# Transposing the first half of even x on TensorE, taking FFN1 part by part, pairing 64-row remainders, moving a diagonal product to VectorE, and loading the gate's x early

## The chip, the cores and the metric

One core of one Trainium2 chip. The metric is the device time of one execution in microseconds (us). Medians are over all runs of a kernel; ratios are explained with the result. "PE" is TensorE (matmuls), "PEld" its weight loads, DVE is VectorE, ACT is ScalarE, POOL is GpSimd, and SP and ACT issue the DMAs. The span of a profile is a little shorter than the time (160.6 us of span for a run of 162.38 us).

## The reference, cut to what matters

```
x: [2048, 448]; g = sigmoid(sum(x * gate_w))          # one gate per row
a = y + x * Dskip        # y: a complex state-space scan, h[t] = Lam*h[t-1] + Bu[t], y = 2 Re(h C)
b = silu(x @ w1) @ w2    # w1: [448, 1792], w2: [1792, 448]
out = g * a + (1 - g) * b
```

448 is 3*128 + 64. So every product that contracts over 448 columns needs three full matmuls and a fourth one with only 64 useful rows, "the remainder". The kernel splits the 2048 rows into even and odd ones. FFN1 (x @ w1, then silu) is done in four chunks of 512 rows: chunks 0 and 1 are even rows, 2 and 3 odd rows. A chunk has 14 blocks of 128 columns of w1.

## The kernel before

The program records operations for each engine with the buffers they read and write, and derives the semaphore waits from them. Each engine runs its own operations in the order given.

```python
# first half of even x: a transposing DMA on SP (XTe0); w1 in column pieces on ACT's queue
ld("act", W1E[:, 0:3, 0:384], ..., "W1Eb")
ld("act", W1E[0:64, 3, :], B_w1[384:448, :], "W1Ea")
...
ldt(XT[:, 0:4, 0:512], x2[0:512, 0:512], "XTe0")
...                                        # later the second half (XTe1), odd x (XTo0, XTo1)
T.op("pool", lambda e: e.memset(W1E[64:128, 3, :], 0.0), writes=["W1Ez"])   # pads the remainder

def ffn1(c, fb, mm_only=False, act_only=None):      # one block, banks 0..3 in turn
    ...
    for j in range(4):                               # j = 3: the remainder, 128 rows of which 64 are zero
        ins = pe.matmul(ps[:, bank, :], W[:, j, fb * 128:(fb + 1) * 128],
                        XT[:, j0 + j, h * 512:(h + 1) * 512], start=(j == 0), stop=(j == 3))
    ...                                              # then ACT: AT = silu(bank)

warm(10)                                             # matmuls on zeros, to bring the clock up
first = [ffn1(0, fb, mm_only=True) for fb in range(2)]
T.op("pe", mm_cols, ...)                             # small vectors into columns, for the P chain on DVE
...
def ytile(kt, odd):                                  # an output tile: 7 matmuls, plus
    if odd:                                          # D*x as a product with diagonal matrices DO
        pe.matmul(ps[:, bank, 0:64], XT[:, 3, t0:t0 + 128], DO[:, 0, 64:128], start=False, stop=False)
        for j in range(1, 4):
            lo = 64 + (j - 1) * 128
            ins = pe.matmul(ps[:, bank, lo:lo + 128], XT[:, 3 + j, t0:t0 + 128], DO[:, j, :], ...)
    ...                                              # DVE: out = bank * g + (1-g)*FFN2
...
# gate: gate_w and all of x are loaded on SP, after the seven LT transposes; 16 reductions on DVE
# order on PE: FFN1 of chunks 0, 1; BU (scan inputs); FFN2 of 0; FFN1 of 2; FFN2 of 1; FFN1 of 3;
#              FFN2 of 2; K0 (needs CO from DVE); FFN2 of 3 and the output tiles
```

Names in the traces: BB and Y hold the rows of B (Y the last 64 of them), LT is B scaled and transposed, BU its product with x, HS the scan's inputs and states. CE and CO are C scaled for even and odd outputs. K0 is CO times BB plus a diagonal of D, by which x enters an even row directly; it is kept in KT. GT is the gate, JK the scratch of its reductions. The P chain is a row of small DVE operations that compute coefficients.

## Time and profile before

| before | |
|---|---|
| time, first median of 3 runs | 161.24 us (161.21 to 162.41) |
| span of the profile | 160.6 us |
| PE busy | 153.4 us, 96% |
| DVE, ACT busy | 68%, 42% |
| PE without a gap | 14.10 to 157.53 us |

The page's engine totals and the shares of the chain of waits (the chain that ended last, followed back):

```profile
PE 153.4 (96%) x772; PEld 73.8 (46%) x772; DVE 108.6 (68%) x216; ACT 67.7 (42%) x111; POOL 7.3 (5%) x16
...
PE 92%; DMA 4%; ACT 2%; DVE 1%; issue 0%
```

PE is the bottleneck, and not only by its share: the chain that ends last is 92% PE. The timeline of PE at the start (start and duration in us, then engine, line, operation, count; in brackets the idle time before and what ended it):

```profile
1.25 4.45 PE L299 MATMUL ps<-Q 128*128 128x512 bf16 x10 [1.25 <-DVE SG L211]
7.13 3.57 PE L275 MATMUL ps<-XT,W1E 128*128 128x512 bf16 x8 [1.43 <-DMA XT<-in_A_x_dram]
10.64 0.25 PE L292 MATMUL ps<-ID,R 3*128 3x3 bf16 x4
10.82 1.90 PE L275 MATMUL ps<-XT,W1E 128*128 128x512 bf16 x8
14.10 20.89 PE L275 MATMUL ps<-XT,W1E 128*128 128x512 bf16 x96 [1.39 <-ACT AT L283]
```

PE waits for x until 7.13 us, its first 8 FFN1 matmuls take 446 ns each, and after 16 it waits for ACT. From 14.10 us it runs at 217.6 ns a matmul (20.89/96). I read the 446 ns, about twice that, as a lowered TensorE clock ("cold"). The profile's granted clock reads 1.00 there, so this is inferred. So the kernel starts "as if" at 14.10 - 16*0.2176 = 10.6 us. I call this the effective start.

The chain of waits in the middle and around the first output tiles (start, duration, what):

```profile
66.74 12.09 PE ps L275 x56
78.83 10.59 PE ps L553 x56
89.42 0.18 PE ps L497 x4
89.60 12.19 PE ps L275 x56
...
122.83 1.32 PE ps L664 x7
124.16 0.03 PE ps L667
124.19 0.17 PE ps L671 x3
```

L275 with 56 matmuls is FFN1 of an odd chunk, L553 the FFN2 between, L497 the columns of D; L664 are the 7 matmuls of an odd tile, L667 and L671 its D*x, 0.20 us. Around the one group of K0 whose weights have only 64 columns, the timeline of PE shows what a change of the array's shape costs:

```profile
116.31 0.22 PE L586 MATMUL ps<-DE,ID 128*128 128x128 bf16 x1
116.46 1.51 PE L584 MATMUL ps<-CO,BB 128*64 128x448 bf16 x7
117.81 0.19 PE L586 MATMUL ps<-DE,ID 128*64 128x64 bf16 x1
117.93 2.82 PE L553 MATMUL ps<-W,AT 128*128 128x448 bf16 x14
```

A 128-column matmul streams for about 0.06 us, yet the next starts 0.15 us later when the shape changes; the 64-column one streams for 0.03 us and the next starts 0.12 us later. That is 0.09 us each way. Last, one of DVE's waits (who waited for whom: us in total, times, longest):

```profile
DVE JK L520 <- DMA W1O<-in_A_x_dram: 7.7, 1, 7.7
```

This is the gate waiting for its x in the middle of DVE's work (33.6 to 41.2 us).

### The profile page before, as it was taken

The page shows a single profiled execution, that of the slowest core. Times are in us where ns is not written, and L with a number is a line of the kernel's source. Part 1 is how long each engine was busy: PE and PEld are TensorE (multiplying, and loading weights), DVE is VectorE, ACT ScalarE, POOL GpSimd, SP SyncE. Part 2 cuts the span into 40 slices and gives each one's busy share as a digit, 9 for nine tenths or more (in the row PEclk, how much of TensorE's full clock was granted, in tenths as well). Part 3 has the DMA queues.
Part 4 walks back from the last instruction along what each step waited for, and adds up shares of the span by engine and source line. Part 5 has one row for each costly group of instructions (what it writes and reads, how often), then busy time and mean ns, then how long its engine had stood idle before and what let it go on. Part 6 is the DMA issues. An engine that isn't in the chain of part 4 may idle for free.

```text
span 160.6 us, 2016 instructions
## 1 busy us (share of the span) xinstructions
PE 153.4 (96%) x772; PEld 73.8 (46%) x772; DVE 108.6 (68%) x216; ACT 67.7 (42%) x111; POOL 7.3 (5%) x16
## 2 busy tenths in 40 slices
PE   6696999999999999999999999999999999999992
PEld 2132444444444455444455444455555555555551
DVE  0027999930799999999999999999941131133341
ACT  3019769999587610766522476331421101100000
POOL 7500000000003000000000000000000000000000
PEclk9999999999999999999999999999999999999999
DMA  5996979799930730026930000000000100102211
GB/s 109 297 354 142 213 142 119 121 149 395 323 82 4 255 145 0 0 63 107 116 69 0 0 0 0 4 2 0 0 0 0 61 30 27 57 0 88 87 57 57
DMA packets 26787, 14.76 MB, mean 92 GB/s; under 512 B 19861, under 2 KB 26010, under 8 KB 26778
## 3 DMA queue, kind: packets, MB, share of 16 engines
q1 hardware_dynamic: 25498, 13.03, 34.3%
q10 hardware_dynamic: 1280, 1.61, 3.3%
q8 instruction: 6, 0.10, 0.2%
q14 instruction: 3, 0.02, 0.0%
HBM read 7.92 MB, written 1.84 MB: 61 GB/s over the span
## 4 chain that ended last, share of the span: by engine, by line
PE 92%; DMA 4%; ACT 2%; DVE 1%; issue 0%
PE ps L275 30%; PE ps L553 26%; PE ps L664 13%; PE ps L569 13%; DMA XT<-in_A_x_dram 4%; PE ps L675 4%; PE ps L584 3%; PE ps L671 1%; ACT L340 1%; ACT P L334 0%; DVE OT L683 0%; ACT AT L283 0%; PE ps L667 0%; ACT JK L340 0%; PE ps L586 0%
## 5 line engine op out<-in xcount | busy, mean ns | idle before, releaser
L553 PE MATMUL ps<-W,AT 128*128 128x448 bf16 x224 | 43.5, 353 | 0.0
L283 ACT ACTIVATE AT<-ps 128x512 bf16<-128x512 f32 x56 | 32.5, 596 | 10.6 <-PE ps L275 10.3
L553 PEld LDWEIGHTS ps<-W,AT 128*128 128x128 bf16 x224 | 21.7, 98 | 20.1 <-issue 0.2
L683 DVE SCALAR_TENSOR_TENSOR OT<-ps,GT,LT 128x448 bf16<-128x448 f32 x16 | 10.9, 684 | 29.0 <-PE ps L675 22.3
L275 PE MATMUL ps<-XT,W1E 128*128 128x512 bf16 x112 | 26.4, 397 | 2.8 <-DMA XT<-in_A_x_dram 1.4
L558 ACT ACTIVATE LT<-ps,GT 128x448 bf16<-128x448 f32 x16 | 9.9, 634 | 43.6 <-PE ps L553 35.3
L275 PE MATMUL ps<-XT,W1O 128*128 128x512 bf16 x112 | 24.5, 379 | 0.0
L569 PE MATMUL ps<-XT,LT 128*128 128x512 bf16 x98 | 21.3, 379 | 0.0
L275 PEld LDWEIGHTS ps<-XT,W1E 128*128 128x128 bf16 x112 | 11.1, 101 | 17.6 <-POOL KT L250 2.3
L275 PEld LDWEIGHTS ps<-XT,W1O 128*128 128x128 bf16 x112 | 10.9, 98 | 12.9
L605 DVE TENSOR_TENSOR_SCAN G<-P,Q 128x1024 f32<-128x1024 f32 x7 | 15.7, 2276 | 0.0
L569 PEld LDWEIGHTS ps<-XT,LT 128*128 128x128 bf16 x98 | 9.6, 98 | 11.6
L520 DVE SCALAR_TENSOR_TENSOR JK<-W1O,GWB 128x448 bf16<-128x448 bf16 x16 | 8.8, 621 | 7.7 <-DMA W1O<-in_A_x_dram 7.7
L664 PE MATMUL ps<-CE,HS 128*128 128x448 bf16 x56 | 11.9, 353 | 0.0
L664 PE MATMUL ps<-CO,HS 128*128 128x448 bf16 x56 | 11.9, 352 | 0.0
L573 ACT ACTIVATE HS<-ps 128x512 bf16<-128x512 f32 x14 | 8.2, 596 | 5.1 <-PE ps L569 4.5
L602 DVE TENSOR_TENSOR Q<-G,SIN 128x1024 bf16<-128x1024 f32 x7 | 8.5, 1219 | 0.0
L602 DVE TENSOR_TENSOR Q<-G,COS 128x1024 bf16<-128x1024 f32 x7 | 8.5, 1210 | 0.0
L664 PEld LDWEIGHTS ps<-CO,HS 128*128 128x128 bf16 x56 | 5.5, 98 | 5.1
L675 PE MATMUL ps<-KT,XT 128*128 128x448 bf16 x32 | 7.4, 352 | 0.0
L664 PEld LDWEIGHTS ps<-CE,HS 128*128 128x128 bf16 x56 | 5.3, 98 | 4.4
L584 PE MATMUL ps<-CO,BB 128*128 128x448 bf16 (+1 forms) x28 | 5.7, 353 | 0.0
(75 smaller groups left out, 110.5 us busy)
## 6 DMA issues: line engine op xcount, KB each, us to landing
W1O<-in_A_x_dram SPq DMA_DIRECT2D x1, 1792.0 KB, 10.3
out_dram<-OT SPq DMA_DIRECT2D x8, 224.0 KB, 1.9
W<-in_B_w_dram SPq DMA_DIRECT2D x1, 1568.0 KB, 13.8
W1O<-in_B_w_dram SPq DMA_DIRECT2D x1, 1344.0 KB, 6.3
W1E<-in_B_w_dram ACTq DMA_DIRECT2D x1, 672.0 KB, 7.8
W1E<-in_B_w_dram ACTq DMA_DIRECT2D x1, 384.0 KB, 6.3
BB<-in_A_B_re_dram SPq DMA_DIRECT2D x1, 336.0 KB, 6.4
BB<-in_A_B_im_dram SPq DMA_DIRECT2D x1, 336.0 KB, 6.9
```

Of the source, the lines that this page charges most:

```text
L275: ins = pe.matmul(ps[:, bank, :], W[:, j, fb * 128:(fb + 1) * 128], XT[:, j0 + j, h * 512:(h + 1) * 512], start=(j == 0), stop=(j == 3))
L283: T.op("act", lambda e: e.activation(a[:, fb, :], ps[:, bank, :], AF.Silu), reads=[f"ps{bank}"], writes=[f"AT{c % 2}_{fb}"])
L520: T.op("dve", lambda e, t=t: e.scalar_tensor_tensor(JK[:, t % 2, :], XN[:, t * D:(t + 1) * D], 1.0, GWB[:, :], ALU.mult, ALU.mult, accum_o ...
L553: ins = pe.matmul(ps[:, bank, 0:D], a[:, fb, q * 128:(q + 1) * 128], W2[:, fb, :], start=(fb == 0), stop=(fb == NFB - 1))
L558: T.op("act", lambda e: e.activation(bs(tile), ps[:, bank, 0:D], AF.Copy, scale=GT[:, 2, tile:tile + 1]), reads=[f"ps{bank}", "GT2"], writ ...
L569: ins = pe.matmul(ps[:, bank, :], LT[:, m, j, :], XT[:, j, h * 512:(h + 1) * 512], start=(j == 0), stop=(j == 6))
L584: ins = pe.matmul(ps[0:M, bank, 0:D], BB[:, m, D + j * 128:D + j * 128 + M], CO[:, m, :], start=(m == 0), stop=False)
L602: T.op("dve", lambda e: e.tensor_tensor(o, a, b, op), reads=reads, writes=writes)
L605: T.op("dve", lambda e: e.tensor_tensor_scan(G[:, c, :], rb, Q1[:, c, :], 0.0, ALU.mult, ALU.add), reads=[f"Q1{c}", "rr"], writes=[f"G{c}"])
L664: ins = pe.matmul(ps[:, bank, 0:D], HS[:, m, o0:o0 + 128], C[:, m, :], start=(m == 0), stop=False)
L675: ins = pe.matmul(ps[:, bank, 0:D], XT[:, j, t0:t0 + 128], KT[:, j, :], start=False, stop=(j == 3))
L683: T.op("dve", lambda e: e.scalar_tensor_tensor(o[:, odd * D:(odd + 1) * D], ps[:, bank, 0:D], GT[:, 1, tile:tile + 1], bs(tile), ALU.mult, ...
```

## The change

Its intent: start FFN1 sooner and without a stall (plain loads of x, transposed by PE; the first seven blocks taken part by part over seven banks); halve the remainders' cost (two remainders on the two halves of the array at once); take D*x of odd rows off PE; and keep DVE out of PE's way (gate's x early, K0 later). All eight banks become one rotation. The diff, cut to its core:

```diff
-        ldt(XT[:, 0:4, 0:512], x2[0:512, 0:512], "XTe0")
+        x0 = x2[0:512, 0:512].rearrange("(k p) c -> p k c", p=128)
+        for i, eng in enumerate(("sp", "act")):     # two plain loads into XH (space of CO)
+            T.dma(eng, ... XH[:, 2 * i:2 * i + 2, :], x0[:, 2 * i:2 * i + 2, :] ...)
+        ld_w("sp", 0)                               # w1 by parts (rows) of K, first 7 blocks
...
+        ld("act", W1E[64:128, 3, :], B_w1[384:448, :], "W1Ez")    # remainder's weights, second copy
-        T.op("pool", lambda e: e.memset(W1E[64:128, 3, :], 0.0), writes=["W1Ez"])
+        swap_xr("pool", 1)                          # XR: x's remainder rows with halves swapped
...
+        def ffn1_mm(c, fbs):                        # groups of up to 4 blocks
+            ...                                     # 3 full matmuls for each block, then
+            def rest(pe):
+                for i, (fb, bank) in enumerate(zip(fbs, banks)):
+                    up = (i % 2 == 1) != bool(odd)
+                    p = slice(64, 128) if up else slice(0, 64)
+                    x = XT[p, 3, hs] if up == bool(odd) else XR[p, hs]
+                    ins = pe.matmul(ps[:, bank, :], W[p, jr, fb * 128:(fb + 1) * 128], x,
+                                    start=False, stop=True)
+        def ffn1_first():                           # 7 blocks, part by part
+            for j in range(4):
+                p = slice(0, 128 if j < 3 else 64)
+                for fb, bank in enumerate(banks):
+                    T.op("pe", ... W1E[p, j, fb*128:...], XT[p, j, 0:512], start=(j==0), stop=(j==3) ...)
-        warm(10)
+        warm(NWARM)                                 # 7; then 16 transposes, 4 copies to XT, 2 to XR
...
+        def skip(kt):                               # DVE: BG = x*g*D, then BG += (1-g)*FFN2
+            ... scalar_tensor_tensor(BG[:, q, :], XO[:, kt, :], GT[:, 1, t:t + 1], DBC[:, :], mult, mult)
+            ... tensor_tensor(BG[:, q, :], BG[:, q, :], bs(t), ALU.add)
-                if odd:                             # the four DO matmuls of ytile
-                    pe.matmul(...)
-        ld("sp", GWB[:, :], ..., "GW")
-        load_xn()
+        ...                                         # the same two loads on ACT, after 7 evictions
-        for j in range(4):
-            k0(j)
+        ffn2(3, 0); ffn2(3, 1)                      # then K0, then ffn2(3, 2), ffn2(3, 3)
```

More of the change, by code (lines that the diff above doesn't have):

```diff
@@ L24 @@
 NKT = 8
+NFA = 7
+NWARM = 7
 class Dma:
@@ L169, in gated_mix @@
         DE = sb("DE", [128, 4, 128], BF16)
-        DO = sb("DO", [128, 4, 128], BF16)
+        DBC = sb("DBC", [128, D], BF16)
+        XR = sb("XR", [128, NK], BF16)
         COS = sb("COS", [128, 4, NK], BF16)
@@ L183, in gated_mix @@
         ID = sb("ID", [128, 128], BF16)
-        R = sb("R", [3, 512], BF16)
-        RD = sb("RD", [2, 512], BF16)
-        PV = sb("PV", [128, 4, 5], F32)
+        R = sb("R", [4, 512], BF16)
+        PV = sb("PV", [128, 4, 4], F32)
         P = sb("P", [128, 48, 4], F32)
@@ L191, in gated_mix @@
         GT = sb("GT", [128, 3, 16], F32)
+        W1EF = W1E[:, :, :].rearrange("p a b -> p (a b)")
+        XO = W1EF[:, 0:NKT * D].rearrange("p (k c) -> p k c", k=NKT)
+        BG = W1EF[:, NKT * D:].bitcast(F32).rearrange("p (k c) -> p k c", k=4)
         LTF = LT[:, :, :, :].rearrange("p a b c -> p (a b c)")
@@ L198, in gated_mix @@
         ps = E(nc.psum_tensor("ps", [128, 8, 512], F32))
-        BK_F1 = [0, 1, 2, 3]
-        BK_F2 = BK_S = [4, 5, 6, 7]
+        BANKS = list(range(8))
         def ld(eng, dst, src, key, group=None):
@@ L208, in ldt, with swap_xr @@
                          writes=[key], group=group)
+        XE = [[f"XTe0{j}" for j in range(4)], ["XTe1"] * 4]
+        def swap_xr(eng, h):
+            hs = slice(h * 512, (h + 1) * 512)
+            T.op(eng, lambda e: e.tensor_copy(XR[64:128, hs], XT[0:64, 3, hs]), reads=XE[h][3:],
+                 writes=[f"XR{h}a"])
+            T.op(eng, lambda e: e.tensor_copy(XR[0:64, hs], XT[64:128, 3, hs]), reads=XE[h][3:],
+                 writes=[f"XR{h}b"])
         T.op("dve", lambda e: e.memset(Q1[:, 0, 0:512], 0.0), writes=["Q10"])
@@ L213, in gated_mix, with ld_w @@
         T.op("dve", lambda e: e.memset(HP[:, :], HALF_PI), writes=["HP"])
-        T.op("pool", lambda e: e.memset(RD[:, :], 0.0), writes=["RD0", "RD1"])
-        gR, gRD, gB = T.group(), T.group(), T.group()
+        gR, gR2, gB = T.group(), T.group(), T.group()
         def row(v):
             return v.rearrange("(o n) -> o n", o=1)
-        ld("act", W1E[:, 0:3, 0:384], B_w1[0:384, 0:384].rearrange("(j p) f -> p j f", p=128), "W1Eb")
+        FA = NFA * 128
+        XH = CO[:, :, :].rearrange("p a b -> p (a b)")[:, 0:2048].rearrange("p (k c) -> p k c", k=4)
+        COK = [f"CO{m}" for m in range(7)]
+        x0 = x2[0:512, 0:512].rearrange("(k p) c -> p k c", p=128)
+        for i, eng in enumerate(("sp", "act")):
+            T.dma(eng, lambda e, i=i: e.dma_start(XH[:, 2 * i:2 * i + 2, :], x0[:, 2 * i:2 * i + 2, :]),
+                  writes=COK[i:i + 1])
+        def ld_w(eng, j):
+            ld(eng, W1E[:, j, 0:FA], B_w1[j * 128:(j + 1) * 128, 0:FA], f"W1Ej{j}")
+        ld_w("sp", 0)
+        for i, (eng, v) in enumerate((("sp", A_log_dt), ("sp", A_Lambda_re), ("act", A_Lambda_im), ("act", A_Dskip))):
+            ld(eng, R[i:i + 1, 0:D], row(v), f"R{i}", gR if i < 2 else gR2)
+        ld_w("act", 1)
+        ld_w("sp", 2)
+        ld("sp", W1E[:, 0:3, FA:], B_w1[0:384, FA:].rearrange("(j p) f -> p j f", p=128), "W1Ed")
         ld("act", W1E[0:64, 3, :], B_w1[384:448, :], "W1Ea")
         T.op("act", lambda e: e.activation(JK[:, 0, 0:1], HP[:, :], AF.Exp), reads=["HP"], writes=["JK0"])
-        ld("act", W1E[:, 0:3, 384:896], B_w1[0:384, 384:896].rearrange("(j p) f -> p j f", p=128), "W1Ec")
-        ld("act", W1E[:, 0:3, 896:], B_w1[0:384, 896:].rearrange("(j p) f -> p j f", p=128), "W1Ed")
-        ldt(XT[:, 0:4, 0:512], x2[0:512, 0:512], "XTe0")
-        for i, v in enumerate((A_log_dt, A_Lambda_re, A_Lambda_im)):
-            ld("sp", R[i:i + 1, 0:D], row(v), f"R{i}", gR)
+        ld("act", W1E[64:128, 3, :], B_w1[384:448, :], "W1Ez")
         ld("sp", BB[:, 0:6:2, D:], A_B_re[0:384, :].rearrange("(t p) d -> p t d", p=128), "Bre", gB)
@@ L250, in gated_mix @@
         T.op("pool", lambda e: e.memset(KT[64:128, 3, :], 0.0), writes=["KTz"])
+        swap_xr("pool", 1)
         SGN = ["SGa", "SGb"]
-        n_f1 = [0]
-        n_f2 = n_s = [0]
-        def nxt(banks, n):
-            b = banks[n[0] % len(banks)]
-            n[0] += 1
-            return b
-        def ffn1(c, fb, mm_only=False, act_only=None):
-            odd, h = c // 2, c % 2
-            bank = nxt(BK_F1, n_f1) if act_only is None else act_only
-            W, j0 = (W1O, 3) if odd else (W1E, 0)
-            a = AT[c % 2]
-            wk = (["W1Oa", "W1Ob", "W1Oz"] if odd else
-                  ["W1Ez", "W1Ea", "W1Eb" if fb < 3 else "W1Ec" if fb < 7 else "W1Ed"])
-            xk = [f"XTe{h}", f"XTo{h}"] if odd else [f"XTe{h}"]
-            def mm(pe):
-                ins = None
-                for j in range(4):
-                    ins = pe.matmul(ps[:, bank, :], W[:, j, fb * 128:(fb + 1) * 128],
-                                    XT[:, j0 + j, h * 512:(h + 1) * 512],
-                                    start=(j == 0), stop=(j == 3))
-                return ins
-            if act_only is None:
-                T.op("pe", mm, reads=wk + xk, writes=[f"ps{bank}"])
-            if mm_only:
-                return bank
@@ new lines, in gated_mix, with nxt, mm @@
+        n_bank = [0]
+        def nxt():
+            n_bank[0] += 1
+            return BANKS[(n_bank[0] - 1) % len(BANKS)]
+        def ffn1_mm(c, fbs):
+            odd, h = c // 2, c % 2
+            hs = slice(h * 512, (h + 1) * 512)
+            W, w0, x0, jr = (W1O, 1, 4, 0) if odd else (W1E, 0, 0, 3)
+            banks = [nxt() for _ in fbs]
+            xk = XE[h] + [f"XTo{h}"] if odd else XE[h]
+            for fb, bank in zip(fbs, banks):
+                def mm(pe, fb=fb, bank=bank):
+                    ins = None
+                    for j in range(3):
+                        ins = pe.matmul(ps[:, bank, :], W[:, w0 + j, fb * 128:(fb + 1) * 128],
+                                        XT[:, x0 + j, hs], start=(j == 0), stop=False)
+                    return ins
+                wk = ["W1Ob"] if odd else ["W1Ej0", "W1Ej1", "W1Ej2"] if fb < NFA else ["W1Ed"]
+                T.op("pe", mm, reads=wk + xk, writes=[f"ps{bank}"])
+            def rest(pe):
+                ins = None
+                for i, (fb, bank) in enumerate(zip(fbs, banks)):
[4 more added lines that the diff above has]
+                                    start=False, stop=True)
+                return ins
+            wk = ["W1Oa", "W1Oz"] if odd else ["W1Ea", "W1Ez"]
+            T.op("pe", rest, reads=wk + xk + [f"XR{h}a", f"XR{h}b"],
+                 writes=[f"ps{bank}" for bank in banks])
+            return list(zip(fbs, banks))
@@ new lines, in ffn1_first @@
+        def ffn1_first():
+            banks = [nxt() for _ in range(NFA)]
+            for j in range(4):
+                p = slice(0, 128 if j < 3 else 64)
+                for fb, bank in enumerate(banks):
+                    T.op("pe", lambda pe, fb=fb, bank=bank, j=j, p=p: pe.matmul(
+                        ps[:, bank, :], W1E[p, j, fb * 128:(fb + 1) * 128], XT[p, j, 0:512],
+                        start=(j == 0), stop=(j == 3)),
+                        reads=[f"W1Ej{j}" if j < 3 else "W1Ea", f"XTe0{j}"], writes=[f"ps{bank}"])
+                if j == 0:
+                    yield
+            nxt()
+            yield list(enumerate(banks))
@@ L283, in ffn1, with ffn1_act @@
+        def ffn1_act(c, fb, bank):
+            a = AT[c % 2]
             T.op("act", lambda e: e.activation(a[:, fb, :], ps[:, bank, :], AF.Silu),
                  reads=[f"ps{bank}"], writes=[f"AT{c % 2}_{fb}"])
-        T.op("dve", lambda e: e.tensor_copy(R[:, D:512], R[:, 384:448]), reads=["R0", "R1", "R2"],
-             writes=["Rd"])
+        def ffn1(c, f0=0):
+            for f in range(f0, NFB, 4):
+                for fb, bank in ffn1_mm(c, list(range(f, min(f + 4, NFB)))):
+                    ffn1_act(c, fb, bank)
+                    yield fb
@@ L289, in mm_cols, with rd @@
+        def rd():
+            T.op("dve", lambda e: e.tensor_copy(R[:, D:512], R[:, 384:448]), reads=["R0", "R1", "R2", "R3"],
+                 writes=["Rd"])
         def mm_cols(pe):
@@ L291, in mm_cols @@
             for pt in range(4):
-                ins = pe.matmul(ps[:, 6, pt * 8:pt * 8 + 3], R[0:3, pt * 128:(pt + 1) * 128],
-                                ID[0:3, 0:3], start=True, stop=True)
+                ins = pe.matmul(ps[:, 7, pt * 8:pt * 8 + 4], R[0:4, pt * 128:(pt + 1) * 128],
+                                ID[0:4, 0:4], start=True, stop=True)
             return ins
@@ L301, in warm, with mm @@
             T.op("pe", mm, reads=["Q10"], writes=["ps7"])
-        warm(10)
-        first = [ffn1(0, fb, mm_only=True) for fb in range(2)]
-        T.op("pe", mm_cols, reads=["R0", "R1", "R2", "Rd", "ID"], writes=["ps6"])
+        warm(NWARM)
+        xp = [ps[:, 3 + j, 0:256].bitcast(BF16) for j in range(4)]
+        for j in range(4):
+            for i in range(2):
+                def mm(pe, j=j, i=i):
+                    ins = None
+                    for k in (2 * i, 2 * i + 1):
+                        ins = pe.transpose(xp[j][:, k * 128:(k + 1) * 128], XH[:, k, j * 128:(j + 1) * 128], ID[:, :])
+                    return ins
+                T.op("pe", mm, reads=[COK[i], "ID"], writes=[f"ps{3 + j}"])
+        for j in range(4):
+            T.op("dve", lambda e, j=j: e.tensor_copy(XT[:, j, 0:512], xp[j]), reads=[f"ps{3 + j}"], writes=[f"XTe0{j}"])
+        T.op("dve", lambda e: e.tensor_copy(XR[64:128, 0:512], xp[3][0:64, :]), reads=["ps6"], writes=["XR0a"])
+        T.op("dve", lambda e: e.tensor_copy(XR[0:64, 0:512], xp[3][64:128, :]), reads=["ps6"], writes=["XR0b"])
+        rd()
+        first = ffn1_first()
+        next(first)
+        T.op("pe", mm_cols, reads=["R0", "R1", "R2", "R3", "Rd", "ID"], writes=["ps7"])
+        first = next(first)
         T.op("dve", lambda e: e.tensor_copy(
-            PV[:, :, 0:3], ps[:, 6, 0:32].rearrange("p (t c) -> p t c", c=8)[:, :, 0:3]),
-            reads=["ps6"], writes=["PV"])
+            PV[:, :, :], ps[:, 7, 0:32].rearrange("p (t c) -> p t c", c=8)[:, :, 0:4]),
+            reads=["ps7"], writes=["PV"])
         names = {}
@@ L493, in side_diag @@
         def side_diag():
-            def mm(pe):
-                ins = None
-                for pt in range(4):
-                    ins = pe.matmul(ps[:, 7, pt * 8:pt * 8 + 2], RD[0:2, pt * 128:(pt + 1) * 128],
-                                    ID[0:2, 0:2], start=True, stop=True)
-                return ins
-            T.op("pe", mm, reads=["RD0", "RD1", "ID"], writes=["ps7"])
-            T.op("dve", lambda e: e.tensor_copy(
-                PV[:, :, 3:5], ps[:, 7, 0:32].rearrange("p (t c) -> p t c", c=8)[:, :, 0:2]),
-                reads=["ps7"], writes=["PVD"])
             for j in range(4):
@@ L506, in side_diag @@
                     DE[:, j, :], ID[:, :], PV[:, j, 3:4], None, ALU.mult),
-                    reads=["ID", "PVD"], writes=[f"DE{j}"])
-                T.op("dve", lambda e, j=j: e.tensor_scalar(
-                    DO[:, j, :], ID[:, :], PV[:, j, 4:5], None, ALU.mult),
-                    reads=["ID", "PVD"], writes=[f"DO{j}"])
+                    reads=["ID", "PV"], writes=[f"DE{j}"])
             yield
@@ L515, in load_xn, with load_xo @@
         def load_xn():
-            ld("sp", XN.rearrange("p (k c) -> p k c", k=NKT), x2.rearrange("(k p) c -> p k c", p=128), "XN")
+            ld("act", XN.rearrange("p (k c) -> p k c", k=NKT), x2.rearrange("(k p) c -> p k c", p=128), "XN")
+        def load_xo():
+            T.dma("sp", lambda e: e.dma_start(XO, x2.rearrange("(k p) c -> p k c", p=128)[:, :, D:]),
+                  writes=["XO", "W1Ez", "W1Ea", "W1Ed", "W1Ej0", "W1Ej1", "W1Ej2"])
+        def skip(kt):
+            t, q = 2 * kt + 1, kt % 4
+            T.op("dve", lambda e: e.scalar_tensor_tensor(
+                BG[:, q, :], XO[:, kt, :], GT[:, 1, t:t + 1], DBC[:, :], ALU.mult, ALU.mult),
+                reads=["XO", "DBC", "GT1"], writes=[f"BG{q}"])
+            T.op("dve", lambda e: e.tensor_tensor(BG[:, q, :], BG[:, q, :], bs(t), ALU.add),
+                 reads=[f"BG{q}", f"BS{t}"], writes=[f"BG{q}"])
         def gate():
@@ L533, in gate @@
                  reads=["GTt"], writes=["GT2"])
-            T.op("pool", lambda e: e.memset(W1O[0:64, 0, :], 0.0), writes=["XN", "W1Oz"])
-            T.dma("sp", lambda e: e.dma_start(W1O[64:128, 0, :], B_w1[0:64, :]), reads=["W1Oz"],
-                  writes=["W1Oa"])
+            XN_DONE = zs
+            for key, p in (("W1Oz", slice(0, 64)), ("W1Oa", slice(64, 128))):
+                T.dma("sp", lambda e, p=p: e.dma_start(W1O[p, 0, :], B_w1[0:64, :]), reads=XN_DONE, writes=[key])
             T.dma("sp", lambda e: e.dma_start(
                 W1O[:, 1:4, :], B_w1[64:448, :].rearrange("(j p) f -> p j f", p=128)),
-                reads=["W1Oz"], writes=["W1Ob"])
+                reads=XN_DONE, writes=["W1Ob"])
             yield
@@ L547, in ffn2 @@
             a = AT[c % 2]
-            bank = nxt(BK_F2, n_f2)
+            bank = nxt()
             def mm(pe):
@@ L563, in bu @@
             pt = m // 2
-            bank = nxt(BK_S, n_s)
+            bank = nxt()
             def mm(pe):
@@ L571, in mm @@
                 return ins
-            T.op("pe", mm, reads=[f"LT{m}", f"XTe{h}", f"XTo{h}"], writes=[f"ps{bank}"])
+            T.op("pe", mm, reads=[f"LT{m}", f"XTo{h}"] + XE[h], writes=[f"ps{bank}"])
             T.op("act", lambda e: e.activation(HS[:, m, 8 + h * 512:8 + (h + 1) * 512],
@@ L577, in k0 @@
         def k0(j):
-            bank = nxt(BK_S, n_s)
+            bank = nxt()
             M = 128 if j < 3 else 64
@@ L655, in ytile @@
             tile = 2 * kt + odd
-            bank = nxt(BK_S, n_s)
+            bank = nxt()
             C, key = (CO, "CO") if odd else (CE, "CE")
@@ L664, in mm @@
                     ins = pe.matmul(ps[:, bank, 0:D], HS[:, m, o0:o0 + 128], C[:, m, :],
-                                    start=(m == 0), stop=False)
-                if odd:
-                    pe.matmul(ps[:, bank, 0:64], XT[:, 3, t0:t0 + 128], DO[:, 0, 64:128],
-                              start=False, stop=False)
-                    for j in range(1, 4):
-                        lo = 64 + (j - 1) * 128
-                        ins = pe.matmul(ps[:, bank, lo:lo + 128], XT[:, 3 + j, t0:t0 + 128],
-                                        DO[:, j, :], start=False, stop=(j == 3))
-                else:
+                                    start=(m == 0), stop=(odd == 1 and m == 6))
+                if not odd:
                     for j in range(4):
@@ L677, in mm @@
                 return ins
-            xk = [f"XTe{kt // 4}", f"XTo{kt // 4}"]
+            xk = XE[kt // 4] + [f"XTo{kt // 4}"]
             T.op("pe", mm, reads=hs_all + [f"{key}{m}" for m in range(7)] + xk
-                 + [f"KT{j}" for j in range(4)] + ["KTz"] + [f"DO{j}" for j in range(4)],
+                 + [f"KT{j}" for j in range(4)] + ["KTz"],
                  writes=[f"ps{bank}"])
@@ L684, in ytile @@
                 o[:, odd * D:(odd + 1) * D], ps[:, bank, 0:D], GT[:, 1, tile:tile + 1],
-                bs(tile), ALU.mult, ALU.add),
-                reads=[f"ps{bank}", "GT1", f"BS{tile}"], writes=[f"OT{kt % 3}_{odd}"])
+                BG[:, kt % 4, :] if odd else bs(tile), ALU.mult, ALU.add),
+                reads=[f"ps{bank}", "GT1", f"BG{kt % 4}" if odd else f"BS{tile}"], writes=[f"OT{kt % 3}_{odd}"])
         outs = []
@@ L698, in chain @@
                 yield from g
-        ld("sp", GWB[:, :], row(gate_w).partition_broadcast(128).rearrange("p o n -> p (o n)"), "GW")
-        load_xn()
         coef = chain(side_coef(), side_diag(), side_C(True), side_C(False))
@@ L708, in run @@
                     break
-        for fb in range(2):
-            ffn1(0, fb, act_only=first[fb])
-        for fb in range(2, NFB):
-            ffn1(0, fb)
+        for fb, bank in first:
+            ffn1_act(0, fb, bank)
+        ld("act", GWB[:, :], row(gate_w).partition_broadcast(128).rearrange("p o n -> p (o n)"), "GW")
+        load_xn()
+        run(ffn1(0, NFA))
         tabs = chain(tables(0), tables(3), tables(1), tables(2))
-        for fb in range(NFB):
-            ffn1(1, fb)
+        for fb in ffn1(1):
             if fb % 3 == 1:
@@ L738, in gated_mix @@
         run(s3)
-        ld("sp", RD[0:1, 0:D], row(A_Dskip), "RD0", gRD)
-        ld("sp", RD[1:2, 64:512], row(A_Dskip), "RD1", gRD)
         load_c()
+        ld("sp", DBC[:, :], row(A_Dskip).partition_broadcast(128).rearrange("p o n -> p (o n)"), "DBC")
+        load_xo()
         run(scan(1))
@@ L749, in gated_mix @@
             ffn2(0, q)
-        for fb in range(NFB):
-            ffn1(2, fb)
+        run(ffn1(2))
         for q in range(4):
@@ L754, in gated_mix @@
         run(coef)
-        for fb in range(NFB):
-            ffn1(3, fb)
+        run(ffn1(3))
         for q in range(4):
             ffn2(2, q)
+        for kt in range(4):
+            skip(kt)
+        ffn2(3, 0)
+        ffn2(3, 1)
         for j in range(4):
             k0(j)
+        ffn2(3, 2)
+        ffn2(3, 3)
         for q in range(4):
-            ffn2(3, q)
             ytile(q, 0)
             ytile(q, 1)
+            skip(q + 4)
             store(q)
```

## The prediction

> **What bounds the kernel now.** TensorE. The page has PE busy 96% of the 160.6 us span; the chain of waits is 92% PE, and from 14.10 us to the last matmul at 157.53 us PE runs without a gap. DVE (68%), ACT (42%) and DMA are covered. A change pays only where it cuts PE time or starts PE's unbroken run sooner.
>
> **The head.** PE waits for the transposing DMA of x until 7.13 us (chain of waits), runs 8 matmuls at 446 ns (cold clock), then stalls 1.39 us because ACT has not emptied the banks (timeline). Steady work costs 217.6 ns per 128x512 matmul (96 in 20.89 us). At 14.10 us 16 matmuls are done, so the start is worth 14.10 - 16*0.2176 = 10.6 us.
> After: plain loads of x (a 288 KB load issued at 0.81 us landed in 3.4 us) arrive about 4.2 us, when the 7 warm-up matmuls end; 16 cold transposes, 2 us; first real matmul about 6.5 us. 28 matmuls over 7 banks run before ACT is needed, so its stall goes. Some 9 matmuls still run cold. Estimated effective start 8.3 us: **-2.3 us**.
>
> **Remainders in pairs.** Each FFN1 block has a fourth matmul with 64 useful rows at full price, 0.216 us. The Trainium skill ("TensorEngine Tiling (Array Packing)", Key Properties) says that tiles on different rows execute in parallel, and that changing tiling mode drains TensorE. No run here shows the first yet. If it holds, 24 pairs each save one matmul: -5.2 us. The second is in the trace: around the one 128x64 group of K0, matmuls start 0.09 us late going in and again coming out (timeline), 0.18 us per excursion. There are 14 groups of remainders, and one in the first part: +2.7 us. Net **-2.5 us**.
>
> **D*x of odd rows leaves PE.** 4 matmuls per odd output tile, 0.20 us in the chain, 8 tiles: **-1.6 us**, all in the final PE-bound stretch. The D-column matmuls (0.18 us plus mode changes) go too: **-0.25 us**. DVE pays about 1.2 us per tile (0.68 us for a 448-column scalar_tensor_tensor, an estimated 0.55 us for an fp32 add, from 1.23 us at 1024) where it is nearly idle.
>
> **Gate's x early.** DVE idles 7.7 us for it (33.6 to 41.2), and CO is ready only 0.9 us before K0 needs it. Loading early moves DVE about 8 us earlier, so PE, some 7 us ahead of before, does not run into it; K0 behind two FFN2 tiles adds 5 us of slack.
>
> **Sum:** 161.24 - 2.3 - 2.5 - 1.6 - 0.25 = 154.6; I say 154.4 us, range 151.5 to 157.2. Faster by over 2%: 0.91; within 2%: 0.08; slower: 0.01.
>
> **What would show it.** First FFN1 matmul at 6 to 7 us; no ACT wait of PE before 20 us. Pairs of 64-row matmuls starting almost together, a group of four costing 0.6 us instead of 0.87. FFN1 on odd rows 11.0 us instead of 12.1. Odd output tiles 1.32 us instead of 1.52. DVE without its gap, PE gap-free.
>
> **What would make it wrong.** If the row halves do not run concurrently, pairing costs 2.7 us and the time is about 159.5. If mode changes are cheaper, 152. If the loads of x share bandwidth with the weights, the head gains nothing; if transposes keep the clock warming, one more us. ACT falling behind in the second chunk could stall PE before BU.

## The result, and the profile after

154.89 us median (154.53 to 155.81, 4 runs) against 161.66 us (161.21 to 162.41, 4 runs): ratio 0.9585, 95% interval 0.9525 to 0.9646, faster. A ratio is the mean time of one kernel's fast runs over that of the other's of the same rounds, so not quite the ratio of the medians quoted. Executions over 1.5% slower than the fastest of the same kernel are left out of the means. The profiled run has a span of 154.1 us.

The page's totals and chain shares, after:

```profile
PE 148.0 (96%) x749; PEld 67.6 (44%) x749; DVE 120.2 (78%) x233; ACT 63.8 (41%) x111; POOL 5.5 (4%) x15
...
PE 91%; DMA 5%; SPq 1%; DVE 0%; issue 0%
```

The timeline of PE at the start:

```profile
1.25 3.17 PE L358 MATMUL ps<-Q 128*128 128x512 bf16 x7 [1.25 <-DVE SG L224]
4.70 1.25 PE L369 MATMUL ps<-ID,CO 128*128 128x128 bf16 x16 [0.28 <-DMA CO<-in_A_x_dram]
5.88 1.46 PE L324 MATMUL ps<-XT,W1E 128*128 128x512 bf16 x6
7.70 0.39 PE L324 MATMUL ps<-XT,W1E 128*128 128x512 bf16 x1 [0.36 <-DVE XR L375]
8.02 0.25 PE L351 MATMUL ps<-ID,R 4*128 4x4 bf16 x4
8.52 1.68 PE L324 MATMUL ps<-XT,W1E 128*128 128x512 bf16 x7 [0.25 <-DMA W1E<-in_B_w_dram]
10.94 3.30 PE L324 MATMUL ps<-XT,W1E 128*128 128x512 bf16 x14 [0.74 <-DMA W1E<-in_B_w_dram]
```

The first FFN1 matmul starts at 5.88 us, on a full clock (1.46 us for six). Then come three new waits: for DVE's swap copies, which still read the seventh block's bank, and twice for parts of w1. The chain of waits has the next work starting at 14.24 us, after 28 matmuls: the effective start is 14.24 - 28*0.2158 = 8.2 us, where 0.2158 us is the steady spacing in this trace (2.59 us for 12 matmuls that follow FFN2).

The chain of one odd chunk of FFN1 (L297 full matmuls, L309 remainders), and of the first output tiles:

```profile
63.33 2.59 PE ps L297 x12
65.92 0.54 PE ps L309 x4
66.45 2.70 PE ps L297 x12
...
74.65 10.70 PE ps L627 x56
...
125.75 2.65 PE ps L738 x14
128.40 0.76 PE ps L742 x4
```

FFN1 of the chunk takes 74.65 - 63.33 = 11.32 us instead of 12.09. What follows a group starts late: twelve full matmuls take 2.70 us after remainders and 2.59 otherwise, and the FFN2 after the chunk 10.70 us instead of 10.59. An odd tile directly follows into the next even one (14 matmuls, 2.65 us, so 1.32 us for the odd tile instead of 1.52). DVE's waits:

```profile
DVE BB L496 <- DMA Y<-in_A_B_im_dram: 5.8, 1, 5.8
...
DVE TMP L483 <- DMA BB<-in_A_B_im_dram: 2.3, 1, 2.3
```

The gate's wait is gone, but two new ones of 8.1 us together stand ahead of it. The one for Y comes from the early load, the one for BB mostly not, as the gate-late run will show. In spans, the 6.5 us are: effective start 10.6 to 8.2, -2.4; chunks 0 and 1 beyond the common part, 17.24 us for what 84 matmuls at the old spacing would take 18.28, -1.0; chunks 2 and 3, -0.77 and -0.78; three late starts of what follows a chunk, +0.3; the D-column matmuls, -0.3; eight odd tiles, -1.6. The sum is -6.6. Both profiled runs lie at the slow end of their kernels' runs (162.38 and 155.81 us).

### The profile page after: what moved, and what is told of

It is laid out like the page before. It is cut to its first block, busy times and chain, and to the rows that moved or that the text cites. A ratio compares the mean times of both kernels' runs of the same rounds, so it can differ in the third digit from the quotient of the medians.

```text
span 154.1 us, 1999 instructions
## 1 busy us (share of the span) xinstructions
PE 148.0 (96%) x749; PEld 67.6 (44%) x749; DVE 120.2 (78%) x233; ACT 63.8 (41%) x111; POOL 5.5 (4%) x15
## 4 chain that ended last, share of the span: by engine, by line
PE 91%; DMA 5%; SPq 1%; DVE 0%; issue 0%
PE ps L627 28%; PE ps L297 21%; PE ps L643 14%; PE ps L738 14%; DMA W1E<-in_B_w_dram 5%; PE ps L309 4%; PE ps L742 4%; PE ps L658 4%; PE ps L324 2%; SPq L208 1%; DVE OT L750 0%; SPq L237 0%; PE ps L660 0%
## 5 line engine op out<-in xcount | busy, mean ns | idle before, releaser
L335 ACT ACTIVATE AT<-ps 128x512 bf16<-128x512 f32 x56 | 29.0, 606 | 13.9 <-PE ps L309 11.9
L297 PE MATMUL ps<-XT,W1O 128*128 128x512 bf16 x84 | 19.5, 380 | 0.0
L297 PE MATMUL ps<-XT,W1E 128*128 128x512 bf16 x63 | 14.6, 380 | 0.0
L750 DVE SCALAR_TENSOR_TENSOR OT<-ps,GT,LT 128x448 bf16<-128x448 f32 x8 | 5.5, 684 | 9.7 <-PE ps L742 9.6
L297 PEld LDWEIGHTS ps<-XT,W1O 128*128 128x128 bf16 x84 | 7.7, 98 | 10.9 <-issue 2.5
L750 DVE SCALAR_TENSOR_TENSOR OT<-ps,GT,W1E 128x448 bf16<-128x448 f32 x8 | 5.5, 684 | 5.1 <-PE ps L738 5.1
L297 PEld LDWEIGHTS ps<-XT,W1E 128*128 128x128 bf16 x63 | 5.7, 98 | 8.6 <-issue 1.7
L324 PE MATMUL ps<-XT,W1E 128*128 128x512 bf16 (+1 forms) x28 | 6.8, 379 | 1.3 <-DMA W1E<-in_B_w_dram 1.0
```

The source lines that it names most:

```text
L297: ins = pe.matmul(ps[:, bank, :], W[:, w0 + j, fb * 128:(fb + 1) * 128], XT[:, x0 + j, hs], start=(j == 0), stop=False)
L324: T.op("pe", lambda pe, fb=fb, bank=bank, j=j, p=p: pe.matmul(ps[:, bank, :], W1E[p, j, fb * 128:(fb + 1) * 128], XT[p, j, 0:512], start=( ...
L335: T.op("act", lambda e: e.activation(a[:, fb, :], ps[:, bank, :], AF.Silu), reads=[f"ps{bank}"], writes=[f"AT{c % 2}_{fb}"])
L750: T.op("dve", lambda e: e.scalar_tensor_tensor(o[:, odd * D:(odd + 1) * D], ps[:, bank, 0:D], GT[:, 1, tile:tile + 1], BG[:, kt % 4, :] if ...
```

## The experiments

Twelve kernels, in four sets; the kernels of a set ran on one chip with runs of the kernel before. All gave correct results. To compare kernels of different sets I use the ratio to the kernel before; the changed kernel had 0.9555 when it was run again (first experiment).

**The changed kernel again** (no edit).

> The changed kernel unaltered, as the reference for the other three of this set on the same chip: 154.5 to 155.5 us, 6 to 7 us below the kernel before.

Measured: 154.95 us median, 0.9555 [0.951, 0.960]. Five fast runs, 154.59 to 155.96. One run, the profiled one, was slow, 159.21 us at a mean clock of 0.989. PE's waits in the first 32 us of that slow run:

```profile
PE ps L298 <- DMA XT<-in_A_x_dram: 2.6, 1, 2.6
```

In that execution the transposing DMA of the second half of even x landed at 21.75 us, after chunk 1 should have begun. I explain no difference between kernels with it, but it shows how little slack that load has.

**Both remainders of a pair on the same half.**

```diff
-                    up = (i % 2 == 1) != bool(odd)
+                    up = bool(odd)
```

> Both matmuls of a pair on the same 64 rows, so nothing can overlap; the same number of matmuls and of mode changes. Theory (the two row halves run at once): 24 pairs cost one matmul more each, 24*0.2157 = +5.2 us over the changed kernel, about 160; FFN1 of an odd chunk 11.32 -> 12.8 us. Rival (the pairs win little by overlap and the trace only shows early starts): no more than +1 us.

Measured: 159.96 us, 0.9853 [0.981, 0.989]. The fast mean is 159.85 against 155.03 of the changed kernel in the same set: +4.8 us. The first odd chunk took 12.8 us, as expected.

**Remainders padded to 128 rows.**

```diff
-                    p = slice(64, 128) if up else slice(0, 64)
-                    x = XT[p, 3, hs] if up == bool(odd) else XR[p, hs]
+                    p = slice(0, 128)
+                    x = XT[p, 3, hs]        # and zeros in the other half of the weights, as before
```

> The remainders as before the change, 128 rows padded with zeros: no overlap and no mode change, the same order and banks as the changed kernel. Theory (each of the 14 groups of remainders pays 0.22 us for going into the 64-row mode and out again, 3.1 us in all): only +2.1 us over the changed kernel, about 157, FFN1 of an odd chunk 12.1 us; and 3.1 us less than the run with both on the same half. Rival (the mode change is free): as slow as the same-half run, +5.2.

Measured: 156.75 us, 0.9659 [0.962, 0.970]; +1.7 us. It also loads 224 KB less at the start, so stages are the cleaner comparison. A group of chunk 2 in the chain of the same-half run, then of the padded run (remainders, then the next twelve full matmuls):

```profile
67.12 0.97 PE ps L309 x4
68.09 2.69 PE ps L297 x12
```

```profile
65.57 0.86 PE ps L308 x4
66.43 2.59 PE ps L297 x12
```

The changed kernel has 0.54 + 2.70 = 3.24 us there, the same-half run 3.66, the padded run 3.45. What follows: the overlap of the two halves is worth 3.66 - 3.24 = 0.42 us for two pairs, one whole matmul each; and going into the 64-row shape and out again costs 3.66 - 3.45 = 0.21 us (0.22 at other groups of these two profiles), half of it ahead of the remainders and half after them. Both rivals fall. Of the 5.2 us that the overlap of 24 pairs gives, about 3 are paid back in changes of shape.

**D*x of odd rows back on PE** (the four DO matmuls restored, skip() removed, a fifth row for the shifted Dskip).

> The odd rows' D*x back on PE as 4 matmuls per odd output tile, the DVE work for it gone. Theory: +1.6 us (8 tiles, 0.20 us each), the output stage 27.28 -> 28.9 us, all else the same. Rival (DVE's added 10 us cost something near the end, so that the move gained less): less than +1 us.

Measured: 157.46 us, 0.9700 [0.966, 0.974]; +2.4 us by the fast means. The two output lines that matter, in its chain:

```profile
127.26 0.03 PE ps L746
127.29 0.17 PE ps L750 x3
```

Its output stage runs from 123.86 to 152.68 us, 28.8 us against 27.3: the expected 1.5 to 1.6. The rest is a flaw of my kernel: it loads Dskip twice more on ACT's queue, and in its profile PE waits 1.1 us, until 9.4 us, for these loads. So the move's worth is 1.6 us, read from the stage, and DVE's added 10 us cost nothing there.

**Gate's loads late** (gate_w and x on SP after the LT transposes, as before the change).

> The changed kernel with only the gate's weights and x loaded late, after the seven transposes as before the change. Theory (needed for the rest): DVE starts the gate some 8 us later (about 47 instead of 39), CO comes 8 us later where K0 has 4.2 us of slack, so PE stalls before K0 for about 4 us: +3 to +4.5 us over the changed kernel, about 158.5. Rival (the early load is without effect, or even in the way of other loads): 0 or a little faster.

Measured: 154.35 us, 0.9536 [0.950, 0.957], all six runs between 154.21 and 154.55. My theory falls. DVE's waits in this run:

```profile
DVE JK L594 <- DMA W1O<-in_A_x_dram: 7.3, 1, 7.3
...
DVE TMP L483 <- DMA BB<-in_A_B_im_dram: 1.6, 1, 1.6
```

The gate's wait is back, the wait of 5.8 us for Y is gone. The gate starts at 40.3 us instead of 39.1, and CO is ready 1.5 us before K0 starts instead of 4.2. The wait for BB is still there (1.6 us, and 2.3 with the early load), so it is mostly not the early load's doing. What the early load did is trade the gate's wait for one for Y: 1792 KB of x, asked for at 14.7 us, share the DMA engines with the small loads of Y, issued from 14.9 us. Y then took 7.2 us from issue to landing (median), here 2.3. The other traces agree. In the six profiles of experiments that ask for x at 13.4 to 14.9 us, Y took 6.5 to 7.0 us; where x is asked for after Y, at 18.5 us (transposing-DMA run) or 20.0 us (block-by-block run), it took 2.2 us and the gate started at 35.8 and 34.9 us, although PE was later. So the step failed by its place among the loads. The changed kernel with x asked for just after Y was not run.

The second half of even x can be late too. POOL's swap copies, which start when it has landed, start at 19.2 us in the changed kernel and at 16.0 us here. In the fast profiles of the same-half, D*x, fewer-excursions and moved-banks runs, which load early, they start between 15.9 and 19.7 us; in the run with fewer excursions PE waited for it.

**The kernel before with the gate's loads early.**

> The kernel before with only the gate's weights and x loaded early, on the ACT queue after the seventh eviction. Theory (worth nothing by itself, since PE there has no gap after 14 us): within 0.3% of the kernel before, with DVE's 7.7 us wait gone from the place and PE still gap-free. Rival: 1 us or more faster.

Measured: 162.57 us, 1.0018 [0.997, 1.007]. Its profile has no wait of DVE for the gate's x, and PE has no gap after 14.93 us. Here x was asked for at 18.1 us, after Y, and the gate did start 6.9 us sooner (34.3 us instead of 41.2). No gain in time is shown, as expected.

**First half of x by the transposing DMA again**, in the changed kernel.

```diff
-        for i, eng in enumerate(("sp", "act")): ...            # plain loads, 16 transposes, copies
-        warm(7)
+        T.dma("sp", lambda e: e.dma_start_transpose(XT[:, 0:4, 0:512], x2[0:512, 0:512]), writes=XE[0])
+        warm(10)
```

> The changed kernel with the first half of even x again by the transposing DMA (and 10 warm-up matmuls as before), the part-by-part order kept. Theory: first FFN1 matmul at about 7.1 us on a cold clock, 28 matmuls done at about 15 us instead of 13.5 to 14.2: +1 to +1.5 us over the changed kernel. Rival (the head's gain comes only from the part-by-part order, or the PE path costs as much as it saves): 0.

Measured: 159.66 us, 0.9876 [0.983, 0.992]: about +5 us, more than three times what I expected. PE at the start:

```profile
9.50 3.17 PE L321 MATMUL ps<-XT,W1E 128*128 128x512 bf16 x7 [3.80 <-DMA W1E<-in_B_w_dram]
12.60 0.26 PE L348 MATMUL ps<-ID,R 4*128 4x4 bf16 x4
12.80 5.26 PE L321 MATMUL ps<-XT,W1E 128*128 128x512 bf16 x21
```

It waits for w1's first part, not for x: that load was issued behind the transpose on SP and landed 7.2 us after its issue. Seven matmuls then ran at about 0.45 us each, which I read as a lowered clock, as above. The rival, that the PE path is without worth, falls. But the experiment mixes two things, the path of x and the place of w1's first part behind it; before the change w1 was on the other queue. How much of the 5 us is x's path alone is not shown.

**The kernel before with 13 warm-up matmuls** instead of 10.

> The kernel before with 13 warm-up matmuls instead of 10, which fill the 1.4 us in which PE waited for x. Rival of the head's explanation (the early start only matters because it keeps the clock up): the first 8 matmuls at 0.24 us instead of 0.45, everything after them 1.5 us earlier, so 1 to 1.7 us below the kernel before. Theory (it is the earlier x and the order): below 0.5 us.

Measured: 161.99 us, 0.9983 [0.994, 1.003]: no gain is shown, though the interval leaves room for 1.0 us; two of six runs slow. PE at the start of its profile reads:

```profile
7.96 1.89 PE L275 MATMUL ps<-XT,W1E 128*128 128x512 bf16 x8 [1.19 <-DMA W1E<-in_B_w_dram]
...
13.25 20.89 PE L275 MATMUL ps<-XT,W1E 128*128 128x512 bf16 x94 [1.39 <-ACT AT L283]
```

The first eight take 0.24 us each instead of 0.45, as the rival has it, and the unbroken run starts 0.85 us sooner in this one trace; the timed runs do not resolve it. A gain of 2.4 us is outside the interval, so the clock alone does not explain the head.

**The first seven blocks block by block**, x still through PE.

```diff
-            for j in range(4):
-                for fb, bank in enumerate(banks): ...
+            for fb, bank in enumerate(banks):
+                for j in range(4): ...
```

> The changed kernel with its first seven blocks block by block, all four parts of one before the next, as before the change; x still transposed on PE. Theory (the part-by-part order hides the landing of the weights behind matmuls that need only the first part): PE waits for the last part, 8 to 10.9 us, before its first block is complete, then the ACT chain: +2 to +3 us over the changed kernel. Rival (the order is of no account, only x counts): under +0.5 us.

Measured: 160.66 us, 0.9861 [0.981, 0.991]: about +5 us, twice the expectation; one of six runs slow. The last of PE's three waits for w1 (1.9 us together), and then the stretches of its start (length in us; busy time and count of PE, PEld, DVE, ACT, POOL; PE clock; DMA share; GB/s):

```profile
9.60 1.79 PE L323 MATMUL ps<-XT,W1E 64*128 64x512 bf16 x5 [0.81 <-DMA W1E<-in_B_w_dram]
```

```profile
8.00:12.00 4.00, 2.79 (x12) 0.89 (x13) 0.17 (x1) 0.16 (x1) 0.00 (x0) 0.81 1.06 262
12.00:16.00 4.00, 4.00 (x10) 0.85 (x9) 2.98 (x22) 3.74 (x10) 0.00 (x0) 0.50 1.12 233
```

PE waits for each part of w1 in turn, and then runs at half its clock: ten matmuls in 4 us. So the order matters more than I had thought: here the gaps came first and a lowered clock after them. All six runs have a mean clock of 0.965 to 0.989, and the fast runs of the repeat 0.997 to 1.0. That the gaps lowered the clock is the likely reading, not tested apart.

**Half as many excursions.** The remainders of two groups run together, the first group's as the end of its sums, the second group's as the start.

```diff
+            main(g1, True); rest(g1, False)           # 3 full matmuls each, then remainders with stop
+            rest(g2, True); main(g2, False)           # remainders with start, then 3 full matmuls each
```

> The remainders of two groups together, as the end of one and the start of the next: 7 excursions into the 64-row mode instead of 14, the same matmuls. Theory (0.22 us per excursion, as the same-half and full-row runs gave): -1.5 us against the changed kernel, about 153.4; FFN1 of an odd chunk 11.32 -> 10.9 us. Rival (what costs is each 64-row matmul, or the first pair of a group, not the change of mode): 0.

Measured: 153.50 us, 0.9462 [0.942, 0.950]; one of six runs slow. The fast mean is 153.53. The ratio is 0.0093 below that of the changed kernel, 1.5 us, as expected. Chunk 2 in its chain:

```profile
62.59 2.59 PE ps L299 x12
65.19 0.97 PE ps L313 x8
66.16 5.29 PE ps L299 x24
```

Eight remainders in 0.97 us: two groups of the changed kernel have 1.08, and the twelve full matmuls in between do not start late. The chunk and the FFN2 after it take 11.01 + 10.59 us instead of 11.32 + 10.70, 0.42 us less for two excursions less. The cost belongs to the change of shape, not to the 64-row matmul. The profiled run is the longest of the fast ones (154.23 us), and in it PE waits for the second half of even x, which landed 15.0 us after its issue:

```profile
19.68 2.76 PE L299 MATMUL ps<-XT,W1E 128*128 128x512 bf16 x12 [1.02 <-DMA XT<-in_A_x_dram]
```

**The same, with the transposes in banks 4 to 7.**

> As the run with fewer switches, and the transposes in the banks 4 to 7 instead of 3 to 6, so that the seventh block's bank does not wait for DVE's two swap copies: another -0.4 us in the head, about 153.0 in all.

Measured: 153.93 us median, 0.9460 [0.941, 0.951]; fast runs 153.04 to 154.52, two of six slow. In the profile the wait for the swap copies of the seventh block is gone, but a wait for DVE of 0.3 us before the column matmuls has come in its place. The expected 0.4 us is not shown.

**The same, with the gate's loads late and K0 one FFN2 tile later.**

> Half the excursions, the transposes in banks 4 to 7, the gate's loads late as in the gate-late run, K0 after three FFN2 tiles of the last chunk instead of two. Theory (the early load of the gate's x delays the transposing DMA of the second half of x, which makes the slow executions): 154.35 of the gate-late run - 1.5 - 0.4 = 152.4 us, all executions within 0.6 us of each other, no wait of PE for x at the start of the second chunk. Rival (the late executions of the two runs with fewer switches come from the reordering itself, or DVE's CO now comes too late for K0): some executions at 155 us or more, or a gap in PE before K0.

Measured: 155.30 us, 0.9569 [0.952, 0.962], 1.8 us worse than the run before it by the ratios; one of six runs slow. My expectation failed. The timeline of PE in chunk 2:

```profile
63.99 0.38 PE L313 MATMUL ps<-XR,W1O 64*128 64x512 bf16 x1
65.94 0.39 PE L313 MATMUL ps<-XT,W1O 64*128 64x512 bf16 x1 [1.57 <-ACT LT L643]
```

The second group's remainders need four more banks at once. These still hold FFN2's results, because ACT scales them by the gate, and the gate's scale is ready at 63.4 us here and at 60.9 us in the run with fewer excursions and early loads. The wait of 1.57 us is most of the loss; K0's later place, changed in the same run, comes after it. So a late gate is free in the changed kernel and costs in this faster one. The runs still spread from 154.63 to 157.07 us, and PE did not wait for x in the profile. With early loads it did, for 1.0 us in a fast run (fewer excursions) and for 2.6 us in the slow run of the repeat. So a late second half of x costs PE time where it happens, but it is not shown to be what makes executions slow; that stays open. The run with fewer excursions is the best version measured, with or without the moved banks.

## Why the prediction was right

The time was forecast at 154.4 and measured at 154.89 us, and the sum was right nearly term by term. The gate's step was wrong, the head was made up otherwise than argued, and two smaller figures were off.

- **The head, -2.3 us.** Profiled: -2.4. The composition was not as predicted. I expected nine matmuls on a low clock; there were none, since the clock was up by 5.9 us. That gain went into the waits for w1's parts and for the swap copies, and the two errors cancel in this profile: that the term fits so well is luck. (The prediction had allowed for it: "if transposes keep the clock warming, one more us".) The same-half run and the slow run of the repeat show a start at about 13.45 instead of 14.24 us, the gate-late run at 12.91, so the gain is 3 us or more in runs whose weights land sooner. "No ACT wait of PE before 20 us" was right. The part-by-part order is needed: without it the time rises by about 5 us. Without x through PE it rises as much, but w1's first part was then held up too, so x's own share is not shown.
- **The pairs, net -2.5 us.** Measured: about -2.3 by stages in the profile, 1.7 by the padded run's time (which starts with less to load). Concurrency is complete: +4.8 us without it, against 5.2 predicted. An excursion costs 0.21 to 0.22 us, not the 0.18 read from the 64-column group. The 11.0 us for an odd chunk did not follow from my own terms: 12.09 - 7*0.216 + 4*0.18 is 11.3, and 11.32 was measured. The Trainium skill ("TensorEngine Tiling (Array Packing)", Key Properties) has both facts, parallel tiles and a drain at each change of mode; these runs agree: two pairs on separate halves save 0.42 us, and a change of shape delays what follows, by 0.21 to 0.22 us there and back.
- **D*x, -1.6, and the D columns, -0.25.** Measured: -1.6 by stage, undone and restored, and -0.3. DVE paid 0.68 + 0.62 us a tile, overlapping to 1.25, where it had room.
- **Gate's x early, "moves DVE about 8 us earlier".** This step failed in the changed kernel. The gate started 2.1 us sooner than before the change and 1.2 us sooner than with late loads, because x, asked for at the same time as Y, made DVE wait 5.8 us for Y. In the kernel before, with x asked for after Y, the gate started 6.9 us sooner, nearly what was forecast. "PE does not run into it" was right even with the late loads: CO still came 1.5 us before K0. What gave that room is worked out, not tested: K0's place behind two FFN2 tiles, 5.3 us of PE work, without which K0 would have come 3.8 us before CO.
- **"ACT falling behind could stall PE before BU"** did not happen: no such wait in the profile.

## What to carry to other kernels

Split small-K matmuls over the two row halves, but count the changes of array shape and put as many small matmuls as possible into one excursion; the second group's small matmuls can open its sums while the first group's close theirs. An earlier load is not a gain until you have read what it delays: here a wait of 7.3 us for the gate's x turned into one of 5.8 for Y, while the same load asked for after Y left DVE no wait for Y or for the gate's x (three profiles). When a start is bound by loads, order the work so that what has landed first is used first: the start with gaps lost 5 us, part of it at a granted clock of 0.50.

## What the Trainium skill lacked or had wrong

- "TensorEngine Tiling (Array Packing)", Key Properties, says that changing the mode drains TensorE, without a figure. Here the delay was 0.09 us each way for a 64-column group and 0.10 to 0.11 us each way for 64-row remainders, 0.21 to 0.22 us per excursion.
- "TensorE: Matmul & The Clock Gate", Part 3, measures row packing with four tiles (3.07 times) and not with two. Here two 64-row matmuls of 512 columns cost one: 0.42 us gained by two pairs, a full factor of 2 less the excursion.
- The same page, Part 4, says that transposes do not count as PE-busy in the same way for the clock. Here 16 transposes of 128x128 took 1.25 us after seven warm-up matmuls (1.96 us in the block-by-block run), and the matmuls after them ran at full speed (six in 1.46 us). This does not contradict the page, since the warm-up came before, but the transposes did not keep the clock from coming up.
- "DMA: Bandwidth & Descriptors" gives a bandwidth for transposing DMAs, and no page gives the time of one whose DMA engines are busy with ordinary loads. The second 512x512 half of x took 8.1 us from issue to landing in the profile of the kernel before, 14.5 us in that of the changed kernel and 11.0 us in that of the run with the gate's loads late. In the four fast profiles with early loads named above it took 11.1 to 15.0 us. These times include waiting behind loads issued before it.
